# One level's mask and the norm's weights moved from VectorE to ScalarE, the last chunk cut, and a new written order

## The chip, the core and the metric

The kernel runs on one core of a Trainium2 chip. The core has a matmul engine (TensorE, PE in the profile, with its weight loads as PEld), three engines that work on elements (VectorE is DVE, ScalarE is ACT, GpSimd is POOL), and queues that start DMA transfers (most on SyncE, SP; some on POOL). Each engine works through its own list of instructions in order, and they wait for one another by semaphores. The metric is the device time of one execution in microseconds (us); a kernel's time is the median of its runs.

## What is computed

Two parts, one feeding the other. The first is a linear recurrence over 768 positions for 4 x 8 independent heads of width 40. The second is a feed-forward block over the 3072 rows that result:

```python
for t in range(S):
    y[:, :, t] = np.einsum('bhd,bhde->bhe', rt, state)
    Sa = np.einsum('bhde,bhe->bhd', state, at)
    state_decay = state * wt[:, :, None, :] - np.einsum('bhd,bhe->bhde', Sa, bt)
    state = state_decay + np.einsum('bhd,bhe->bhde', vt, kt)
...
rms = np.sqrt(np.mean(x * x, axis=-1, keepdims=True) + 1e-06)
xn = x / rms * rms_g
g = xn @ w_gate
silu = g * (1.0 / (1.0 + np.exp(-g)))
val = xn @ w_val
return silu * val @ w_out
```

The output `y` at position t reads the state before position t is added, so the state after the last position is never read. The rows of x are 320 wide (8 heads of 40), the hidden width is 1536. All data is fp32 on the chip; the weights arrive as 64-bit floats and are converted there.

## The kernel before

**Chunks.** The 768 positions are cut into 24 chunks of 32 (`C`, `NCH`). All 32 heads are worked on together: partitions hold heads and positions, the free dimension holds 16 groups (`NI`) of them. For each chunk c there are three stages.

- `front(c)` (line 676) loads w, a, k, b and v of the chunk, transposes them on PE, and builds for levels of 1, 2, 4, 8 and 16 positions (`LEVELS`) the decayed keys `K`, the decayed factors `Ab` and the products between positions, which masked copies put into `LT`. At the end (lines 775 to 777) it transposes `K` once more, 8 transposes, and ACT copies the result into `KN[32]`, the keys for the update of the state. It also sends `LT` to DRAM and back in another layout, as `M`.
- `inverse(c)` (line 780) solves the triangular system of the chunk on DVE, in 31 pairs of small instructions on `tmp` and `Yi` (62 on DVE for each chunk), and returns the result to `LT` by two DMA steps through `sY`.
- `main(c)` (line 800) uses the state `ST` and the chunk's `LT`: it forms `X`, then the solved values `U`, which go into `VU`; `Sdec` (line 813, 128x640 on DVE) is the decayed state, the 32 products called "update" (line 823) are the new contribution to it, and their sum is the next `ST`. Then come the scores `sc` (32 products, in PSUM), which are masked for each level into `As` (lines 853 to 862), multiplied with the keys of that level (`level`), and combined on DVE from the largest level down into `y` (`down`). Then `y` is transposed, normed (a Square with a sum, a power on POOL, a scaling on ACT), transposed again in three pieces, and written to `xg` with the norm's weights `gcol` (line 920).

The mask `msi` of a level says for each of two halves i of the partitions which positions count. For the largest level (G == 1) and the smallest (l == 1) one DVE instruction on 128x512 elements does both halves, for the three levels between two instructions of 128x256. At the largest level the mask of a half has the same value at all 16 positions.

**Groups.** Two chunks make a group of 64 positions in 4 batches, 256 rows (`CG`, `GT`). `feed(g)` (line 922) is the feed-forward block on a group: 12 slices of 128 hidden columns are loaded (`wf`, by SP), and for each slice PE makes gate and value products into `ps` (of the 320 rows of weights the last 64 by "h64", which needs the third piece of `xg`, the first 256 by "h"), ACT applies Silu (`sg`), DVE multiplies (`hT`), and PE multiplies with the output weights into `po`.

**Weights.** `narrow(f, h)` (line 956) converts the 64-bit weights in 24 half slices at the start, on DVE and ACT, and stores them in DRAM (`sW`), from where every `feed` loads them.

**Order.** What each engine does is not left to a scheduler. All stages only record pieces (a PE piece is a set of products, on other engines a piece is one instruction) in a `Plan`. `Plan.issue` (line 347) then walks through `ORDER`, a text of 6407 words: a number is the place of the next piece among those not yet issued, and "-" stands for one filler, a 128x128 product of the identity into an unused part of `po` (line 1000), which keeps PE's clock up in the first part of the program. `PAIRS` says for each PSUM result which of three buffers `ps` it uses. Each engine's list is its pieces in this order, so the text decides what waits behind what on each engine and on the SP and POOL queues. The two texts were found by a search outside the program; `PRODUCTS`, `LOADS` and the durations in `dve`, `scalar` and so on (in us) are what it planned with.

In the profile nearly all instructions carry the line of a helper: L475 is any DVE instruction, L498 a Silu or other function on ACT, L502 a copy on ACT, L505 a scaling on ACT, L508 the power on POOL, L518 a DMA, L521 a product, L524 a transpose, L1000 a filler.

Of the kernel before, what the change touches and what calls it, by code (L numbers as in the profile page):

```python
# [7 lines left out]
FP32 = mybir.dt.float32  # L8
# [8 lines left out]
P = 128  # L17
C = 32
LEVELS = (1, 2, 4, 8, 16)
CG = 2  # L20
WB = 5
S0, S1 = 15.0, 2.0
LEAD = 2
WARM = 230.0
# [21 lines left out]
36 33 2 26 42 1 31 0 25 343 37 29 107 38 24 36 26 34 262 2 13 1 35 40 0 190 24 339 13 14 - - - 40 17 44 15 41 43 55  # L46
42 8 60 47 175 72 48 45 84 185 59 68 186 585 54 58 - - - - - 49 93 586 53 179 69 71 599 81 176 57 597 50 67 178 609
70 188 80 622 51 92 16 623 65 610 52 56 177 633 64 66 - - - - - - - - - - - - 61 189 9 598 77 79 187 78 587 620 62 0
587 81 - - - - 72 75 179 82 62 90 595 384 194 588 87 11 633 89 589 74 395 620 197 590 380 88 73 195 391 - - - - 101
196 209 390 610 84 102 214 381 201 611 202 5 212 86 213 383 591 85 0 222 92 591 611 17 95 221 224 223 384 94 234 225  # L50
- - 197 233 237 93 391 245 246 592 328 393 198 598 645 612 0 641 598 15 612 592 - 338 205 206 380 642 599 209 0 207
612 200 0 337 612 186 598 6 326 613 2 599 641 34 176 200 216 217 23 600 389 215 33 201 355 95 202 177 96 214 - - - -
211 187 339 93 0 577 0 561 578 297 579 171 192 53 187 191 - - - 182 188 200 623 172 185 625 186 580 562 581 612 355
582 199 1065 197 583 611 183 198 624 184 0 152 1005 850 298 0 298 0 837 295 0 0 0 83 130 298 148 0 298 83 0 507 307
833 0 303 555 0 840 307 0 290 0 67 125 316 314 0 132 125 67 0 0 131 314 0 286 325 0 130 0 298 130 0 291 292 - - - -
- 287 0 293 0 304 0 316 305 301 0 0 283 0 296 0 311 0 322 281 0 286 0 295 280 0 292 - - - - - - - - - - - - - - - -
- 288 0 0 0 0 301 0 285 62 301 116 305 0 283 250 116 0 - - - - - - - - 293 0 258 112 296 0 110 300 256 0 308 307 245
293 292 0 0 304 0 288 0 301 - - - - - - 298 306 0 0 313 0 297 0 0 0 293 310 494 301 0 494 0 302 0 0 299 492 0 0 296
0 246 0 791 0 0 0 787 0 0 93 468 2 796 94 469 0 94 462 794 0 467 93 94 290 461 95 462 96 468 511 97 469 291 98 470
481 289 99 292 471 0 99 100 101 471 102 472 103 481 511 104 482 105 488 106 489 107 483 2 490 108 109 0 293 109 490  # L60
0 108 0 0 379 0 379 387 0 387 369 0 405 378 387 406 0 - - - - - - - - - - - - - - - - - - - - - - - - - - - - - - -
- - - - - - - - - - - - - - - - - - - - - - - - - - - - - - - - - - - - - - - - 44 0 367 377 0 415 0 42 0 414 383 43
412 0 383 410 0 383 40 373 0 0 0 0 0 0 36 0 377 - - - - - - - - - - - - - - - - - 44 0 377 35 44 0 414 0 0 82 0 32 -
43 0 373 0 90 0 229 407 38 88 0 40 78 226 42 38 41 47 48 0 43 226 42 50 45 48 396 0 50 396 43 0 396 0 0 379 395 380
0 395 380 0 401 0 394 0 378 242 400 44 0 400 47 0 145 45 377 242 0 145 391 377 0 216 1 145 391 42 635 398 429 626
146 0 397 39 145 426 634 398 146 147 631 43 623 44 621 45 632 46 148 47 622 - - - - 639 375 376 149 48 416 239 641
830 150 399 377 640 840 0 150 641 653 48 838 151 658 152 645 828 - - - - - - 642 153 670 154 646 155 682 49 656 50
156 669 657 51 157 666 158 667 52 159 643 668 - - - - - - - 53 389 160 161 678 162 1 651 652 - 647 2 702 655 3 654 0
594 610 611 609 625 595 636 109 608 110 596 373 - - - - - - - - - - - 605 590 374 111 345 783 607 626 782 383 112
627 620 622 385 793 113 623 606 375 382 114 792 621 - - - - - - - 617 384 115 376 346 116 377 619 117 635 634 118  # L70
618 378 119 - - - - - 160 633 120 379 121 163 380 161 122 381 123 162 124 164 386 - - - - - - - - - 629 125 387 126
127 128 388 129 630 130 640 631 389 638 131 390 - - - - - 167 641 132 391 133 639 134 392 168 135 393 - - - - - 165
136 394 137 138 430 139 166 571 431 581 643 140 - - - 171 721 644 580 141 642 142 570 143 174 645 144 173 145 178 -
- - 182 175 146 177 147 172 150 149 179 - - - 180 148 637 176 185 732 432 186 433 0 1065 584 283 - 39 1064 36 582 38
284 638 37 40 635 583 0 17 635 480 625 567 497 40 18 624 498 41 284 568 626 42 285 499 627 43 570 286 642 636 44 500
2 706 287 45 643 897 0 493 500 501 643 287 897 656 644 648 2 45 597 907 502 649 494 0 457 860 458 0 613 0 457 611
552 0 - 596 457 621 598 0 622 0 456 595 610 853 457 622 458 634 854 0 505 - - - 500 360 765 521 361 449 531 519 764
504 532 543 362 508 363 0 500 517 543 501 4 515 363 502 364 506 419 514 365 5 366 516 367 0 367 419 368 421 369 370
420 422 44 0 370 - 430 371 44 0 3 40 0 367 426 368 369 370 504 371 37 372 373 374 375 429 376 526 525 521 377 505
522 0 338 466 390 339 397 377 9 340 391 341 392 342 430 393 398 343 480 440 400 378 439 395 387 429 396 394 403 408  # L80
388 0 403 0 342 474 700 403 578 0 700 403 342 709 490 343 0 474 7 696 405 343 709 475 403 344 0 487 706 472 0 485
695 10 343 704 404 0 404 0 4 404 37 405 0 401 31 337 481 402 45 0 474 3 337 338 41 339 402 0 42 3 0 398 705 399 471
50 335 400 898 336 703 470 401 337 37 907 338 339 402 27 480 699 908 704 340 403 341 897 479 486 701 889 343 700 584
478 890 713 714 481 899 702 719 28 706 559 900 342 712 29 560 731 30 0 531 9 0 9 683 684 17 10 0 10 454 0 450 552 10
451 0 10 672 0 672 - - - - - - - - - - - - - - - - 662 25 0 27 670 26 0 682 680 24 695 539 677 676 678 704 661 37 -
- - - 3 36 675 662 296 4 681 434 691 663 679 692 703 672 5 0 0 428 1 680 683 42 682 666 43 687 681 667 20 40 686 21
677 695 2 22 292 0 675 705 287 0 675 287 688 0 671 0 669 665 269 7 17 410 8 682 29 411 412 30 667 413 414 0 8 665 0
675 8 681 672 9 674 0 9 672 - - - - - - - - - - 481 0 9 37 483 411 0 471 0 25 5 401 6 402 403 404 471 7 39 405 473 -
- - - - - - - - - - - 16 0 0 28 8 27 397 0 397 28 0 397 0 654 462 0 5 396 36 8 397 398 37 399 14 47 462 15 0 457 10
723 44 3 11 43 458 583 644 21 12 646 582 4 13 645 461 0 571 21 13 572 458 393 22 14 394 15 466 0 391 455 19 0 372 0  # L90
16 436 0 694 28 5 27 442 6 695 371 439 7 0 696 0 451 370 435 6 760 0 745 0 428 0 741 362 425 0 751 433 362 741 0 748
362 0 425 423 358 733 0 358 0 744 358 432 359 360 0 427 428 0 7 359 0 359 15 0 359 360 6 0 425 0 428 442 359 360 361
362 363 364 0 360 361 742 362 0 362 363 364 419 365 742 366 367 2 368 423 751 369 370 371 372 373 424 675 374 7 0
424 2 0 1154 672 0 1154 421 422 732 432 738 0 669 730 1002 732 670 420 995 731 439 742 685 985 421 0 993 421 687 735
422 686 743 4 1002 423 748 736 991 424 746 983 366 757 367 759 368 425 992 369 744 0 369 746 371 757 755 370 759 768
425 767 736 582 0 582 3 583 584 0 584 751 0 582 746 774 0 731 0 431 737 731 747 421 745 0 731 364 580 0 580 739 581
582 439 583 584 2 424 585 740 757 0 759 740 753 754 760 585 755 586 750 366 587 424 588 365 589 425 364 590 419 591
363 752 592 593 0 347 174 346 175 331 176 342 177 0 177 178 0 178 7 179 342 180 181 359 182 8 183 184 185 186 187
188 189 12 341 190 352 191 192 349 193 194 350 224 195 196 351 0 222 9 224 5 0 4 217 7 0 214 328 335 218 16 332 226
219 343 344 0 417 223 267 338 182 224 266 183 13 184 276 185 0 183 222 184 274 185 186 223 187 330 188 20 189 338 0  # L100
229 223 0 223 188 189 190 191 226 194 227 192 3 225 229 193 224 239 4 0 231 4 0 228 7 233 193 234 238 235 338 339
236 340 532 341 239 12 530 240 194 241 533 195 242 541 197 243 0 538 240 9 608 10 241 536 338 4 13 339 527 242 340
192 539 243 341 342 343 244 0 339 340 240 341 342 0 538 342 240 343 0 16 343 324 344 539 737 345 346 538 727 540 552
# [290 lines left out]
def kernel(  # L394
# [41 lines left out]
    N = 8  # L436
# [116 lines left out]
    for j, l in enumerate(LEVELS):  # L553
        nc.vector.tensor_scalar(iw[:, 2], iw[:, 0], j, None, ALU.logical_shift_right)
        nc.vector.tensor_scalar(msk[:, j], iw[:, 2], 1.0, None, ALU.is_equal)
# [477 lines left out]
```

## Time and profile before

| | |
|---|---|
| median of 5 runs | 1110.35 us (1106.63 to 1112.51) |
| the profiled execution: its time | 1110.35 us |
| its span, from first to last instruction | 1108.5 us |
| granted PE clock, mean over the span | 0.978 |
| products of the first group end, of the last group begin | 265 us, 1062 us |

| row of the profile | count | mean |
|---|---|---|
| DVE As<-ps,msi 128x512 (two levels) | 48 | 683 ns |
| DVE xg<-ps,gcol 128x384 | 24 | 562 ns |
| DVE Sdec<-ST,T 128x640 | 23 | 821 ns |
| PE ps<-ident,K 128x128, all / busy | 192 | 26.4 us |
| PE ps<-VU,KN 64x40, all / busy | 1536 | 20.5 us |
| ACT KN<-ps 128x640 | 96 | 692 ns |
| ACT sg<-ps 128x256 | 144 | 383 ns |
| ACT x<-ps,ss 128x320 (scaled by a column) | 24 | 530 ns |
| ACT Xs<-ps 128x320 (scaled by a number) | 24 | 436 ns |
| PE po<-ident 128x128 (fillers) | 560 | 73.5 us busy |

Each fp32 product is two passes on PE, so a set of 32 products shows as 64, and 280 fillers as 560. A row's busy time is the time in which at least one of its instructions ran; the mean is that of one instruction from start to end, and neighbours overlap. The profile's "idle before" of an engine says how long it stood before such an instruction and which instruction released it. The granted clock is what the throttle allowed PE: 1.00 is full speed, 0.50 half.

### The profile page before, as it was taken

What the parts mean: (1) busy time and instruction counts of PE and PEld (TensorE: products, weight loads), DVE (VectorE), ACT (ScalarE), POOL (GpSimd) and SP (SyncE); (2) the same over time, 40 slices, a digit from 0 to 9 for tenths busy, and PEclk for the clock granted to TensorE, in tenths of its full rate; (3) what the DMA queues carried; (4) which work ended last, traced back from release to release, by engine and by line L of the source; (5) the groups of instructions that cost most, each with busy time, mean ns of one, the idle gap of its engine ahead of it and who ended that gap; (6) DMA issues with size and microseconds to landing.
All of it is one profiled execution on the core that took longest, in us unless ns stands there. A gap on an engine that the chain in (4) does not pass through costs nothing.

```text
span 1108.5 us, 53122 instructions
## 1 busy us (share of the span) xinstructions
PE 1044.8 (94%) x23152; PEld 863.6 (78%) x23152; DVE 906.8 (82%) x3065; ACT 454.5 (41%) x989; POOL 303.2 (27%) x534
## 2 busy tenths in 40 slices
PE   5798889989999999999999999999999999999998
PEld 5697777877878877877777887877878788888876
DVE  5999999899798889789799689989878889798421
ACT  4645554644235235335335335335325335332211
POOL 7520344022223412413422422422304312200000
PEclk9798999989999999999999999999979999999999
DMA  7635554775545636546535545535536535434242
GB/s 158 151 75 155 132 118 123 197 225 142 156 118 128 154 102 145 130 119 153 126 96 142 146 110 150 140 95 153 119 108 149 126 108 151 108 107 130 80 141 79
DMA packets 171177, 145.43 MB, mean 131 GB/s; under 512 B 123712, under 2 KB 142080, under 8 KB 170944
## 3 DMA queue, kind: packets, MB, share of 16 engines
q1 hardware_dynamic: 152576, 119.06, 39.2%
q0 software_dynamic: 16192, 22.64, 10.0%
q8 instruction: 182, 2.98, 1.2%
q10 hardware_dynamic: 2176, 0.33, 0.2%
q14 instruction: 51, 0.42, 0.1%
HBM read 125.83 MB, written 16.12 MB: 128 GB/s over the span
## 4 chain that ended last, share of the span: by engine, by line
PE 64%; DVE 23%; ACT 4%; DMA 3%; issue 3%; POOL 1%; SPq 1%; DVEq 0%; ACTq 0%; POOLq 0%
PE ps L521 43%; PE po L521 11%; PE ps L524 9%; DVE LT L475 3%; DVE tmp L475 3%; DVE Yi L475 3%; DVE K L475 2%; DVE As L475 2%; DVE ex L475 1%; DMA sY<-Yi 1%; DVE wf L475 1%; DVE y L475 1%; ACT K L502 1%; DVE r L475 1%; DVE Ab L475 1%
## 5 line engine op out<-in xcount | busy, mean ns | idle before, releaser
L521 PE MATMUL ps<-xg,wf 128*128 128x256 f32 (+1 forms) x1728 | 357.7, 395 | 2.6 <-DVE xg L475 1.6
L521 PEld LDWEIGHTS ps<-xg,wf 128*128 128x128 f32 (+1 forms) x1728 | 263.2, 190 | 58.1 <-issue 15.2
L521 PE MATMUL po<-wf,hT 128*128 128x320 f32 x576 | 178.6, 444 | 2.9 <-DVE hT L475 1.8
L475 DVE TENSOR_TENSOR tmp<-Yi,M 128x60 f32<-128x60 f32 (+24 forms) x744 | 156.4, 210 | 19.4 <-DMA M<-sB 3.1
L475 DVE TENSOR_TENSOR Yi<-Yi,tmp 128x60 f32<-128x60 f32 (+24 forms) x744 | 155.7, 209 | 15.9
L498 ACT ACTIVATE sg<-ps 128x256 f32<-128x256 f32 x144 | 53.7, 383 | 239.9 <-PE ps L521 222.4
L518 POOL DMA_DIRECT2D VU<-in_v_dram x92 | 53.4, 587 | 354.9 <-PE ps L524 208.2
L521 PEld LDWEIGHTS po<-wf,hT 128*128 128x128 f32 x576 | 102.2, 190 | 39.0 <-issue 3.4
L475 DVE TENSOR_TENSOR hT<-ps,sg 128x256 f32<-128x256 f32 x144 | 59.4, 420 | 54.9 <-ACT sg L498 53.5
L475 DVE TENSOR_TENSOR K<-K,T 128x512 f32<-128x512 f32 (+1 forms) x192 | 93.4, 495 | 10.5 <-PE ps L521 3.8
L521 PEld LDWEIGHTS ps<-Ab,K 40*64 40x64 f32 x4608 | 78.4, 140 | 29.0 <-issue 9.1
L521 PE MATMUL ps<-Ab,K 40*64 40x56 f32 x4608 | 88.3, 226 | 9.4 <-DVE LT L475 2.7
L502 ACT COPY K<-K 128x256 f32<-128x256 f32 (+1 forms) x168 | 71.3, 443 | 61.2 <-PE ps L521 39.6
L475 DVE TENSOR_TENSOR As<-ps,msi 128x256 f32<-128x256 f32 (+1 forms) x192 | 83.3, 482 | 13.0 <-PE ps L521 12.8
L502 ACT COPY KN<-ps 128x640 f32<-128x640 f32 x96 | 66.4, 692 | 55.1 <-PE ps L524 21.6
L521 PEld LDWEIGHTS ps<-As,KN 128*40 128x40 f32 x3072 | 67.1, 125 | 17.4 <-issue 9.4
L521 PE MATMUL ps<-As,KN 128*40 128x32 f32 x3072 | 74.2, 206 | 5.1 <-issue 2.2
L1000 PE MATMUL po<-ident 128*128 128x128 f32 x560 | 73.5, 285 | 5.3 <-ACT po L544 5.3
L518 POOL DMA_DIRECT2D kbn<-in_b_dram x92 | 53.8, 587 | 83.6 <-PE ps L521 73.0
L518 POOL DMA_DIRECT2D wn<-in_w_dram x92 | 51.8, 568 | 85.7 <-DVE tmp L475 32.5
L518 POOL DMA_DIRECT2D kbn<-in_k_dram x92 | 53.4, 584 | 74.3 <-PE ps L521 73.6
L1000 PEld LDWEIGHTS po<-ident 128*128 128x128 f32 x560 | 68.1, 198 | 6.7 <-POOL wan L514 5.2
(124 smaller groups left out, 1549.8 us busy)
## 6 DMA issues: line engine op xcount, KB each, us to landing
wf<-sW SPq DMA_DIRECT2D x144, 480.0 KB, 4.0
M<-sB SPq DMA_DIRECT2D x96, 128.0 KB, 3.8
rn<-in_r_dram SPq DMA_DIRECT2D x24, 160.0 KB, 4.3
sW<-ex SPq DMA_DIRECT2D x16, 240.0 KB, 3.3
out_dram<-o SPq DMA_DIRECT2D x48, 80.0 KB, 3.4
kbn<-in_b_dram POOLq DMA_DIRECT2D x92, 40.0 KB, 3.6
wan<-in_w_dram POOLq DMA_DIRECT2D x46, 80.0 KB, 3.1
wan<-in_a_dram POOLq DMA_DIRECT2D x46, 80.0 KB, 3.3
```

Of the source, the lines that this page charges most:

```text
L475: plan.add("DVE", time + more + each * size(o), 0.087, lambda at: fn(at(o), *m(at)), [o], aps(*args))
L498: scalar(o, [a], lambda at: nc.scalar.activation(at(o), at(a), f, **kw), aps(acc), 0.1 if f in (AF.Square, AF.Relu) else 0.0)
L502: scalar(o, [a], lambda at: nc.scalar.copy(at(o), at(a)), extra=more)
L518: plan.add(by, 0.6 if by == "POOL" else 0.45, 0.0, lambda at: queue.dma_start(out=o, in_=i), [o], [i], load=LOADS[load], since=since)
L521: return o, lhsT, rhs, lambda at: nc.tensor.matmul(at(o), lhsT, rhs, start=start, stop=stop, skip_group_check=True), 4
L524: return o, i, ident, lambda at: nc.tensor.transpose(at(o), i, ident), 2
L1000: plan.warm = lambda: nc.tensor.matmul(po_[:, 0, DM:DM + P], ident, ident, start=False, stop=False, skip_group_check=True)
```

## The change

The masks of the largest level are made by two ACT scalings, one for each half, with one mask value per partition as the factor, in place of one DVE product. The norm's weights are applied by three ACT scalings (one for each piece of 128 columns) in place of one DVE product. In the last chunk, whose new state nobody reads, the 8 transposes and the copy for `KN[32]`, `Sdec` and the 32 update products are no longer recorded. `ORDER` has 6472 words in place of 6407, among them 277 fillers in place of 280, and nearly every line of it is another; `PAIRS` is new too.

There is also a second way of solving the chunk's system in two blocks of 16, used for chunks below `BLOCKS`; `BLOCKS` is 0, so nothing of it is recorded but the constant `lower` (one DVE instruction on 128x1 at the start), and it is cut from the diff here.

```diff
+BLOCKS = 0
...
 ORDER = """
-36 33 2 26 42 1 31 0 25 343 37 29 107 38 24 36 26 34 262 2 13 1 35 40 0 190 24 339 13 14 - - - 40 17 44 15 41 43 55
...
 PAIRS = """
...
@@ front
-        z["KN"][32] = KN_[32].next()
-        copy(z["KN"][32].rearrange("p (n o e) -> p n o e", n=N, o=2),
-             turned(K.rearrange("p (n i) x s -> p n (i x s)", i=2)).rearrange("p n (o e) -> p n o e", o=2)[:, :, :, 0:D])
+        if c + 1 < NCH:
+            z["KN"][32] = KN_[32].next()
+            copy(z["KN"][32].rearrange("p (n o e) -> p n o e", n=N, o=2),
+                 turned(K.rearrange("p (n i) x s -> p n (i x s)", i=2)).rearrange("p n (o e) -> p n o e", o=2)[:, :, :, 0:D])
...
@@ main
-        if c > 0:
+        if 0 < c < NCH - 1:
             tt(Sdec, ST.rearrange("p n i d -> p (n i) d")[:, :, 0:D], z["T"][32].to_broadcast((P, NI, D)), MUL)
...
-        up = plan.room()
-        pe("update", [mm(up[part(o), i, col(slot(n))], kn(z, 32, i, n, o), VU[half(i), n, o, 0:D]) for n, i, o in each])
+        if c + 1 < NCH:
+            up = plan.room()
+            pe("update", [mm(up[part(o), i, col(slot(n))], kn(z, 32, i, n, o), VU[half(i), n, o, 0:D]) for n, i, o in each])
...
-            if G == 1 or l == 1:
-                tt(As[:, j], sc.rearrange("p o n t -> p (o n) t")[:, :, None, 1 if l == 1 else 16:C:2 if l == 1 else 1].to_broadcast((P, NI, 2, 16)),
+            if G == 1:
+                for i in range(2):
+                    scale(As[:, j, :, i], sc.rearrange("p o n t -> p (o n) t")[:, :, 16:C], msi[:, j, i, 0:1])
+            elif l == 1:
+                tt(As[:, j], sc.rearrange("p o n t -> p (o n) t")[:, :, None, 1:C:2].to_broadcast((P, NI, 2, 16)),
                    msi[:, j:j + 1].to_broadcast((P, NI, 2, 16)), MUL)
...
-        tt(xg[c // CG][:, :, c % CG * P:(c % CG + 1) * P], ps, gcol[:, :, None].to_broadcast((P, KT, P)), MUL)
+        for kt in range(KT):
+            scale(xg[c // CG][:, kt, c % CG * P:(c % CG + 1) * P], ps[:, kt], gcol[:, kt:kt + 1])
```

## The prediction

> **What bounds the kernel now.** I read the page's shares first, then the chain that ended last, then the engines in three stretches, then what PE and DVE wait for, and last the one place where PE's clock falls in mid-run.
>
> ```profile
> PE 1044.8 (94%) x23152; PEld 863.6 (78%) x23152; DVE 906.8 (82%) x3065; ACT 454.5 (41%) x989; POOL 303.2 (27%) x534
> PE 64%; DVE 23%; ACT 4%; DMA 3%; issue 3%; POOL 1%; SPq 1%; DVEq 0%; ACTq 0%; POOLq 0%
> ```
>
> PE is busy 94% of the span and carries 64% of the chain, DVE 23%. Those are averages over stretches with different limits, so the span is cut where the first group's products end (265) and where the last group's begin (1062):
>
> ```profile
> 0.00:265.00 265.00, 224.44 (x4868) 196.41 (x4868) 235.43 (x761) 137.78 (x272) 94.28 (x178) 0.94 0.57 149
> 265.00:1062.00 797.00, 779.10 (x18093) 636.24 (x18092) 666.01 (x2293) 311.42 (x705) 208.91 (x356) 0.99 0.49 127
> 1062.00:1108.50 46.50, 41.28 (x192) 30.99 (x192) 5.33 (x13) 5.31 (x14) 0.00 (x0) 0.99 0.36 111
> ```
>
> The columns after the length are PE, PEld, DVE, ACT and POOL busy, then granted clock. In the first stretch PE's 224 contain the 73.5 us of fillers (the row of L1000), and DVE with 235 of 265 is the full engine. In the second PE idles 797 - 779.1 = 17.9 us; DVE has 84%, ACT 39%. In the third PE is alone.
>
> ```profile
> PE ps L521 <- issue: 4.7, 10, 0.9
> PE ps L521 <- DVE LT L475: 2.2, 3, 1.4
> PE ps L524 <- DVE tmp L475: 1.1, 2, 0.6
> PE ps L521 <- DVE xg L475: 1.0, 1, 1.0
> PE ps L521 <- ACT KN L502: 0.9, 2, 0.5
> ```
>
> These are PE's longest waits between 265 and 1062 (total, times, longest). All the rows that name DVE sum to 6.3 us, those that name ACT to 3.8. No single wait is worth much.
>
> ```profile
> 809.82 2.24 DVE L475 COPY_PREDICATED LT<-near,ps 128x384 f32<-128x384 uint32 x3
> ...
> 812.11 1.16 PE L521 MATMUL ps<-Ab,K 40*64 40x56 f32 x64 [1.45 <-DVE LT L475]
> ...
> 800.00:820.00 20.00, 17.83 (x420) 14.44 (x420) 17.18 (x60) 6.62 (x15) 1.02 (x2) 0.86 0.32 102
> 820.00:840.00 20.00, 19.91 (x434) 16.16 (x427) 13.35 (x46) 4.93 (x13) 6.46 (x12) 0.80 0.45 103
> ```
>
> PE stands 1.45 us behind three masked copies on DVE, then 0.19 and 0.53 more, and in rows of 2 us the granted clock is 0.58 at 814 to 816 and 0.50 from there to 828: some 13.6 us at half speed, which cost 13.6 x 0.5 = 6.8 us. It is the only such stretch after 265.
>
> **The change part by part.** Counted in the order of both programs: DVE's recorded instructions go from 3043 to 2994 (24 for the mask, 24 for the norm's weights, one Sdec), ACT's from 968 to 1087 (48 + 72, less one KN copy), and on PE one set of 32 update products and one of 8 transposes are gone. No DMA is added or removed. ORDER and PAIRS are replaced whole, so every queue's sequence moves; SP keeps its 712 transfers and POOL its 460. On SP a weight load that waits for a buffer holds back the LT loads behind it: PE waited 1.4 us for LT<-sY before 265 and not at all after, and I add nothing for a new sequence (the same 1.4 each way).
>
> *Work removed from PE.* In the last chunk 8 transposes of K go (row ps<-ident,K: 26.4 us / 192 x 8 = 1.10 us) and 64 passes of ps<-VU,KN (20.5 / 1536 x 64 = 0.85 us). Both stood between 959 and 1040, where PE idles almost nowhere: -1.95 us. It could shrink to 0 only if PE found nothing ready in their place, and group 10's products are.
>
> *DVE relieved.* Per chunk the 128x512 mask (683 ns) and the 128x384 weights (562 ns): 1.245 us. Up to 265 four chunks' shares go, 5.0 us, from the engine that is full there. The ends are -5.0 (all of it on the path) and +0.5: DVE's waits for ACT in this stretch are 15.2 us, 7.4 of them one early wait, and the other 7.8 grow with ACT's added 8.5 us on 137.8 (6%). The chain there runs through DVE, ACT, DMA and issue by turns, and the PE work ahead of the last filler is the same in both orders (110 us by the trace's durations) with 277 fillers in place of 280, which speaks for little; I take half, -2.5.
> From 265 to 1062 twenty chunks' shares and Sdec (0.82) go: 25.7 us, by which DVE's 131 us of idle time grow by a fifth. PE's waits for it (6.3 us) can fall by nothing or by all; I take the same fifth, -1.3.
>
> *ACT loaded.* A scaling by a column costs 530 ns for 320 elements (x<-ps,ss) against 436 by a number (Xs<-ps), so 94 ns more. A half of the mask, 256 elements, is then 383 + 94 = 0.48, and a third of the weights, 128 elements, 0.30 + 0.09 = 0.39 (Ab<-Ab, 296 ns). Neighbours overlap by 0.1 (two K copies of 0.40 take 0.71), so the mask is 0.86 us against DVE's 0.68, and the weights 0.97 against 0.56. Per chunk that is 0.96 + 1.17 = 2.13 us of ACT, 42.6 us on 311 in the middle stretch (14%).
> For the mask the path hardly changes: between the score products and the first level products the new PE order holds at least 1.8 us of other PE work, as the old one did, and a median of 4.7. If that cover were gone it would cost 0.18 a chunk. For the weights the cover is thin. Between a group's last transposes of x and its first product the old order held 0.0 to 5.6 us of PE work, and 0.0 at two groups, where PE waited (xg: 1.6 us in 2 waits, one ahead of the last group). The new order has no group at 0.0, but eight of twelve at 0.8 to 1.2, against a chain of 0.97. The ends are -1.6 (both waits gone, none new) and 8 x 0.4 = 3.2 less 1.6, or +1.6; I take -0.2. PE's other waits for ACT, 3.8 us, grow with its load: 14%, +0.5 (ends 0 and +3.8).
> What is queued behind the new instructions on ACT are the copies of K, KN and Ab and the activations sg; PE waits for KN, hT and K through them. ACT stood idle 61% of the middle stretch, 181 us of it behind PE for sg, which is the cover.
>
> The Trainium skill speaks against this move: "ScalarE: Activation LUTs", section "Rules for kernel authors", gives multiplications to VectorE. The rows agree on each duration (0.97 against 0.56, 0.86 against 0.68). By the rule the change would lose (0.41 + 0.18) x 24 = 14 us if all were on the path; by the load of the two engines it loses none of that.
>
> *The clock.* A new order has new gaps. The half-speed stretch can vanish (-6.8) or be joined by another (+6.8). I take the fifth by which DVE's slack grows, -1.4. The rule in "TensorE: Matmul & The Clock Gate", section "What's actually happening", is that the clock halves after an idle window of about 3.4 us. Here it fell after 2.2 us of idling in pieces, so the row is stricter than the rule. By the rule no order that keeps PE this full would halve it, and the sum would have -6.8 here.
>
> *Sum.* The profiled execution took 1110.35 us, span 1108.5 and 1.85 around it, and it is also the median of the five runs (1106.63 to 1112.51). -1.95 - 2.5 - 1.3 - 0.2 + 0.5 - 1.4 = -6.85, so 1103.5 us.
>
> **The rivals.** *More half-clock stretches (slower).* Place: the middle stretch, wherever the new order leaves PE some 2 us without work. Price: 6.8 for the clock and 2.2 for the gaps, 9.0 each. From 1103.5 + 1.4, one more than before gives 1113.9 and two 1122.9; I write 1118. It decides from the first extra one. For it: a single wait of 1.45 was enough, and every gap is new. Against: DVE, which made that gap, gets lighter.
> *ACT's queue becomes the wait (slower).* The new scalings wait on PE at ACT's head and hold back a copy of 0.40 in each chunk: 24 x 0.40 = 9.7 us against -1.95 and -2.5, so 1115.6. For it: ACT waits for PE longer than for anything else, and it works in order. Against: 61% idle, and at least 1.8 us of cover at the mask.
> *DVE was never the limit (same).* Only PE's removed work comes out: 1110.35 - 1.95 = 1108.4. For it: the middle stretch is PE's, and the fillers are nearly as many. Against: DVE at 89% up to 265, 23% of the chain.
> That the change does less than it says can be left aside: BLOCKS is 0, so the block inverse is not recorded, and the counts above are those of the words.
>
> **How the numbers follow.** Forecast 0.56, more half-clock 0.22, ACT's queue 0.08, DVE no limit 0.14. The predicted time is the forecast's 1103.5. Its own range is 1095 (start 5.0, all DVE waits, half the clock stretch: -1.95 - 5.0 - 6.3 - 3.4 = -16.6, with +1.2 for ACT) to 1109. The range given is 1095 to 1117, which takes in the ACT case and one extra stretch and leaves out two, and about a tenth below. What a measurement can tell from no change is about 0.3%, 3.3 us: faster is below 1107.0, slower above 1113.7. Faster: 0.53 from the forecast, 0.05 from the PE-only case, 0.58. Slower: most of the clock's 0.22 and half of ACT's, 0.26. The rest, 0.16, is same.
>
> **What would show it.** In the new profile: DVE busy near 907 - 30.7 = 876, ACT near 454.5 + 51 - 0.7 = 505, and PE near 1042. Up to the end of the first group's products (265 before) the start should take about 262; if it still takes 265, DVE was no limit there. PE's waits for xg should be small and many, not two large ones, and now name ACT. The granted clock between 265 and 1062 should dip once or not at all. What would make this wrong: a second or third dip there, PE idle in the middle stretch above 20 us, or waits of PE for ACT of 10 us and more.

## The result and the profile after

The changed kernel took 1112.99 us (median of 53 runs, 1103.83 to 1119.16), the kernel before on the same chips 1109.27 us (95 runs): a ratio of 1.0032, 95% interval 1.0021 to 1.0043. It is 3.7 us slower, where 6.85 us less had been forecast. The profiled execution of the changed kernel took 1110.23 us (span 1108.1, mean granted clock 0.983), 2.8 us under its own median: over its 54 recorded executions 0.01 of mean clock goes with 6.5 us (7.5 us for the kernel before), and at a clock of 0.98 the two stand at 1113.2 and 1109.7 us. The two profiled executions took the same time, so the traces show what is different inside, not the 3.7 us.

The page of the changed kernel: engine shares, the DMA queue of kind "instruction" (packets, MB, share), and the chain's shares by engine:

```profile
PE 1041.3 (94%) x23074; PEld 858.7 (77%) x23074; DVE 887.5 (80%) x3017; ACT 487.4 (44%) x1108; POOL 302.7 (27%) x534
...
q8 instruction: 181, 2.97, 1.1%
...
PE 65%; DVE 20%; issue 5%; ACT 4%; DMA 3%; POOL 2%; SPq 1%; DVEq 0%; POOLq 0%; ACTq 0%
```

DVE lost 19.3 us of busy time (the instructions that went had 30.7 us of durations, all durations together fell by 28.4; overlaps make the rest), PE 3.5. On the chain DVE gave up 3 points, and "issue" took 2 of them. The three stretches of the changed kernel, columns as before:

```profile
0.00:265.00 265.00, 221.21 (x4856) 193.54 (x4857) 232.79 (x749) 141.78 (x292) 93.92 (x178) 0.95 0.58 149
265.00:1062.00 797.00, 778.85 (x18032) 634.38 (x18031) 649.80 (x2257) 339.85 (x803) 208.75 (x356) 0.99 0.50 127
1062.00:1108.10 46.10, 41.25 (x188) 30.82 (x188) 4.91 (x12) 5.77 (x14) 0.00 (x0) 0.97 0.37 110
```

PE's busy time in the middle is what it was (778.85 against 779.1), though the last chunk's work is gone from it. PE's longest waits there, changed kernel:

```profile
PE ps L524 <- issue: 8.1, 11, 1.9
PE ps L524 <- DVE Yi L478: 1.5, 3, 0.7
PE po L524 <- issue: 1.3, 1, 1.3
PE ps L524 <- DVE hT L478: 0.8, 2, 0.6
PE ps L524 <- DVE tmp L478: 0.7, 2, 0.5
```

The rows that name DVE now sum to 4.6 us (6.3 in the prediction's count), those that name ACT to 3.0; the rows with no releaser, "issue", grew from 6.0 to 9.4. The clock dips after 265 are three short ones (10.2 us at half speed in all, near 774, 785 and 819) in place of one of 13.7. The first two follow at once on waits of PE with no releaser (1.94 us before 774.1, 1.11 before 784.1). The first group's products end at 266.8 (265.2 before).

The largest new hole lies in the start. The stretch around 200 in the kernel before, then in the changed kernel (us, then PE, PEld, DVE, ACT, POOL busy, granted clock, DMA share, GB/s):

```profile
197.00:200.00 3.00, 3.00 (x29) 3.00 (x28) 2.50 (x6) 2.75 (x6) 0.00 (x0) 1.00 0.60 178
200.00:203.00 3.00, 2.89 (x78) 2.62 (x76) 2.97 (x9) 1.38 (x5) 0.00 (x0) 1.00 0.69 210
203.00:206.00 3.00, 3.00 (x18) 2.13 (x16) 2.90 (x9) 0.12 (x1) 0.00 (x0) 1.00 0.35 90
```

```profile
197.00:200.00 3.00, 0.04 (x2) 0.00 (x0) 2.68 (x7) 2.19 (x4) 0.00 (x0) 1.00 0.90 275
200.00:203.00 3.00, 2.28 (x78) 2.10 (x78) 2.56 (x8) 0.89 (x2) 0.00 (x0) 0.66 0.61 183
203.00:206.00 3.00, 3.00 (x14) 2.00 (x12) 2.97 (x9) 1.41 (x5) 0.00 (x0) 0.50 0.58 168
```

PE stands for 3 us, and then its clock is halved for 7 us. What it waits for is the subject of the last experiments.

### The profile page after: what moved, and what is told of

It reads as the page before. It is cut to its first block, busy times and chain, and to the rows that moved or that the text cites. A ratio compares the mean times of both kernels' runs of the same rounds, so it can differ in the third digit from the quotient of the medians.

```text
span 1108.1 us, 53038 instructions
## 1 busy us (share of the span) xinstructions
PE 1041.3 (94%) x23074; PEld 858.7 (77%) x23074; DVE 887.5 (80%) x3017; ACT 487.4 (44%) x1108; POOL 302.7 (27%) x534
## 3 DMA queue, kind: packets, MB, share of 16 engines
q8 instruction: 181, 2.97, 1.1%
## 4 chain that ended last, share of the span: by engine, by line
PE 65%; DVE 20%; issue 5%; ACT 4%; DMA 3%; POOL 2%; SPq 1%; DVEq 0%; POOLq 0%; ACTq 0%
PE ps L524 44%; PE po L524 12%; PE ps L527 8%; DVE tmp L478 3%; DVE LT L478 3%; DVE Yi L478 3%; DVE ex L478 2%; DVE y L478 2%; DVE K L478 2%; DVE As L478 1%; DVE wf L478 1%; SPq L521 1%; DVE Ab L478 1%; POOL kbn L521 1%; DMA wf<-in_moe_w_out_dram 1%
## 5 line engine op out<-in xcount | busy, mean ns | idle before, releaser
L521 POOL DMA_DIRECT2D VU<-in_v_dram x92 | 53.3, 586 | 363.9 <-PE ps L527 229.3
L505 ACT COPY KN<-ps 128x640 f32<-128x640 f32 x95 | 65.6, 692 | 55.5 <-PE ps L527 21.4
L521 POOL DMA_DIRECT2D kbn<-in_b_dram x92 | 53.6, 586 | 99.6 <-PE ps L524 99.6
L524 PEld LDWEIGHTS ps<-As,KN 128*40 128x40 f32 x3072 | 64.8, 123 | 18.1 <-issue 13.9
L478 DVE TENSOR_TENSOR As<-ps,msi 128x256 f32<-128x256 f32 (+1 forms) x168 | 68.5, 455 | 11.0 <-PE ps L524 8.9
L524 PE MATMUL ps<-As,KN 128*40 128x32 f32 x3072 | 71.5, 204 | 4.1 <-issue 3.0
L521 POOL DMA_DIRECT2D wn<-in_w_dram x92 | 51.6, 566 | 86.6 <-DVE KN L478 39.1
L521 POOL DMA_DIRECT2D kbn<-in_k_dram x92 | 53.7, 587 | 51.1 <-PE ps L524 43.6
```

Source lines behind the costliest of these rows:

```text
L478: plan.add("DVE", time + more + each * size(o), 0.087, lambda at: fn(at(o), *m(at)), [o], aps(*args))
L505: scalar(o, [a], lambda at: nc.scalar.copy(at(o), at(a)), extra=more)
L521: plan.add(by, 0.6 if by == "POOL" else 0.45, 0.0, lambda at: queue.dma_start(out=o, in_=i), [o], [i], load=LOADS[load], since=since)
L524: return o, lhsT, rhs, lambda at: nc.tensor.matmul(at(o), lhsT, rhs, start=start, stop=stop, skip_group_check=True), 4
```

## The experiments

Names: b_ kernels are the kernel before with an edit, n_ kernels the changed kernel with one. A part that is added or undone is put into the written order at the place of the instruction that it replaces; all else keeps its place. Ratios are against the kernel before on the same chip, with 95% intervals.

**Each part undone in the new order.**

```diff
 n_maskdve: the changed kernel, the mask of the largest level on DVE
-for i in range(2): scale(As[:, j, :, i], ...sc[16:C], msi[:, j, i, 0:1])
+tt(As[:, j], ...sc[16:C].to_broadcast(...), msi[:, j:j + 1].to_broadcast(...), MUL)
 n_xgdve: the norm's weights on DVE
-for kt in range(KT): scale(xg[...kt...], ps[:, kt], gcol[:, kt:kt + 1])
+tt(xg[...], ps, gcol[:, :, None].to_broadcast((P, KT, P)), MUL)
 n_order: both
```

> The changed kernel with its new order, but the largest level's mask is again one DVE product (at the place of the first of its two ACT scalings). Theory M (the mask's scalings on ACT lose: ACT and DVE read the same PSUM buffer one at a time, in the changed trace ACT stands 28.8 us behind DVE's masks): the loss of 3.7 us goes, about 1107 us, ratio 0.997 to 1.000 to the kernel before. Theory O (the new order itself loses): stays near 1113, ratio 1.002 to 1.004. Theory X (the norm's weights on ACT lose): stays near 1113. ACT's waits for DVE's As fall to 0 in any case.

> The changed kernel with its new order, but the norm's weights are again one DVE product (at the place of the first of the three ACT scalings). Theory X: back to 1109 or below. Theories M and O: stays near 1113, ratio 1.002 to 1.004.

> The changed kernel's order and shortened last chunk, with both the mask and the norm's weights back on DVE. Theories M and X: 1106 to 1109, that is the kernel before less the 1.95 us of PE work. Theory O: 1112 or more. If DVE's relief was worth something in this order, this is slower than the one with only the mask put back.

Measured: n_maskdve 1.0092 [1.0063, 1.0121], n_xgdve 1.0076 [1.0051, 1.0101], n_order 1.0147 [1.0118, 1.0176]. In the new order each part on ACT is worth having: 0.6% for the mask, 0.44% for the weights, 1.15% for both. None of the theories had expected n_maskdve and n_xgdve above 1113 us. So the loss against the kernel before is not in the two moves as such; the order, with the work where it was, is 1.5% worse. That is a price for work which this order was not made for; the same work in both orders is compared further down.

**Each part alone in the old order.** The same edits on the kernel before, forwards; b_cut is only the shortened last chunk, b_all all three.

> The kernel before with its own order and only the last chunk shortened (8 transposes, a KN copy, Sdec and 32 update products left out; their words taken out of the order). All theories: PE loses 1.95 us of work, so 1107 us, ratio 0.998. If it stays at 1109 the removed work was filled by idling.

> The kernel before with its own order and only the largest level's mask as two ACT scalings (at the place of the DVE product). In the new order this mask on ACT is worth 6.7 us (0.32% against 0.92%). Theory O (the parts gain, the new order loses): 1102 to 1107, ratio below 0.998. Rival F (an order fits the engines it was found for, any single move loses in it): ratio above 1.002, since ACT's queue has no room made for it.

> The kernel before with its own order and only the norm's weights as three ACT scalings (at the place of the DVE product). Theory O: below 0.998. Rival F: above 1.002; two groups have no PE work between the last transposes and the first product, so PE's waits for xg grow by 0.4 us at each.

> The kernel before with its own order and all three parts: mask and weights on ACT, last chunk shortened. This is the change without the new order. Theory O: 1098 to 1104, ratio 0.990 to 0.995. Rival F: 1112 or more. DVE busy near 887, ACT near 487 as in the changed kernel.

Measured: b_cut 0.9991 [0.9969, 1.0014], b_mask 1.0033 [1.0012, 1.0053], b_xg 1.0040 [1.0015, 1.0064], b_all 1.0088 [1.0065, 1.0111]. The cut gives about 1 us or nothing. In an order that was not made for them, both moves lose, as rival F had it. For the weights PE's waits show it; the longest between 265 and 1062 in b_xg:

```profile
PE ps L519 <- ACT xg L503: 4.8, 10, 1.1
PE ps L519 <- DVE LT L473: 2.2, 3, 1.4
```

All of PE's waits for ACT after 265 grew from 3.8 to 10.2 us. For the mask it is ACT and DVE that wait for one another. In b_mask, among DVE's and ACT's own waits:

```profile
DVE As L473 <- ACT As L503: 22.1, 21, 4.0
ACT As L503 <- DVE As L473: 15.0, 12, 2.0
```

and in the changed kernel, where ACT's turn comes after DVE's:

```profile
ACT As L508 <- DVE As L478: 28.8, 19, 4.6
```

DVE was to save 16 us by the mask; in b_mask it stands 22 us for ACT (its waits for PE at the masks fall from 12.8 to 7.3). In none of the 24 chunks of the changed kernel do the two engines' masks overlap, though they work on different levels; in 21 chunks one engine begins 0.03 to 0.10 us after the other's end.

**Why the two take turns.** Both read the scores in PSUM and write parts of one tile `As`. n_sep writes the largest level into a tile of its own.

```diff
-As_ = Turns(1, [P, len(LEVELS), NI, 2, 16], "As")
+As_ = Turns(1, [P, len(LEVELS) - 1, NI, 2, 16], "As")
+As16_ = Turns(1, [P, NI, 2, 16], "Ah")
...
-scale(As[:, j, :, i], ...)
+scale(Ah[:, :, i], ...)
```

> The changed kernel with the largest level's mask written to a tile of its own, the others to theirs. If ACT waits for DVE's masks because they write one tile, the 28.8 us of waiting vanish; if because both read one PSUM buffer, they stay and so does the time, near 1113 (ratio 1.003).

> The changed kernel unaltered, beside the kernel before on one chip. The variant with a tile of its own for the largest mask has the same instructions and waits as this and measured 0.9998. If the kernel's loss holds on any chip: ratio 1.002 to 1.004. If chips differ: 0.998 to 1.001.

Measured: n_sep 0.9998 [0.9973, 1.0023], the changed kernel unaltered once more (after_again) 1.0023 [1.0005, 1.0042]. ACT's waits in n_sep:

```profile
ACT Ah L508 <- DVE As L478: 28.7, 19, 4.6
```

The wait is the same, so it is not the written tile. What the two engines still share is the PSUM buffer `sc` and the table of masks `msi`; no run separates these. n_sep has the changed kernel's instructions and nearly its waits, so it is a second sample of it, and the gap between its ratio and the 1.0032 says what twelve runs can tell. The Trainium skill has a rule that points to `sc`: "PSUM — Partial Sum Buffer", section "PSUM bank collisions raise a hardware error", says that two engines may not be on the same bank and quadrant at once, two reads included, and that the compiler keeps them apart by a dependency. The waits here agree with it.

**The mask left out.** After the first chunk the largest level is not masked anew: b_nomask in the old order, n_nomask in the new one.

```diff
 b_nomask
-tt(As[:, j], ...sc[16:C].to_broadcast(...), msi[:, j:j + 1].to_broadcast(...), MUL)
+if c == 0: tt(As[:, j], ...sc[16:C].to_broadcast(...), msi[:, j:j + 1].to_broadcast(...), MUL)
 n_nomask
-for i in range(2): scale(As[:, j, :, i], ...)
+for i in range(2 if c == 0 else 0): scale(As[:, j, :, i], ...)
```

> The kernel before in its own order, the largest level's mask left out from the second chunk on (23 DVE products of 0.683 us gone, nothing put on ACT; that level's product then reads the first chunk's masked scores). What freeing DVE of the mask is worth at most. If DVE limits: 16 us less DVE work gives 1100 to 1106. If PE limits and DVE's relief is worth nothing: 1108 to 1110, ratio 0.998 to 1.001.

> The changed kernel in its order, with the largest level's mask left out from the second chunk on (46 ACT scalings gone; that level's product reads the first chunk's). What the two scalings and ACT's 29 us of waiting behind DVE's masks cost in the changed kernel. If they are its loss: 1108 to 1109 or less, ratio below 1.000. If they are hidden: as the changed kernel beside it, within 1 us.

Measured: b_nomask 0.9973 [0.9952, 0.9994], n_nomask 1.0031 [1.0016, 1.0047]. With 16 us less on DVE the old order gains 3.0 us. In the new one, leaving out ACT's scalings and their 28.8 us of waiting gains nothing against after_again: there they are covered, as the prediction had it.

**The same work in two orders.** b_neither and n_neither have the cut, no mask of the largest level after the first chunk and no weights after the second group: every engine has the same work but for 3 of 280 fillers (0.8 us). nb_start has n_neither's order up to the end of the first group's products and b_neither's after it, nb_half up to the fifth group. b_tail is b_cut with the new order from the middle of group 9 on.

```diff
 b_neither, n_neither: beside the mask as in b_nomask
-tt(xg[...], ps, gcol[...], MUL)
+if c < 2 * CG: tt(xg[...], ps, gcol[...], MUL)
 nb_start, nb_half
+order of n_neither: pieces 0 to the end of the first group's products (nb_start), or through the fifth group (nb_half)
+order of b_neither: all pieces not yet issued, as they stand there
```

> All work on the engines of the kernel before, last chunk shortened, its own order up to the middle of group 9's products and the new order for what is left after that. In the traces the stretch after group 10's last product is 44.9 us in the new order and 47.0 in the old. So 1.95 and 2.1 us less: 1105 us, ratio 0.996. If the shorter end is paid for before it: 0.998 to 1.000, as with the last chunk shortened alone.

> Old order, with both moved pieces of work left out of the kernel before: the largest level's mask from the second chunk on, the norm's weights from the third group on (the later groups' products read old rows), and the last chunk shortened. What is left on every engine is the same as in the next run. With the mask left out the old order measured 0.9973; less the cut's 0.1% and less the waits for the weights: 1103 to 1106, ratio 0.993 to 0.996.

> The new order, with the same work left out (largest mask from the second chunk on, norm's weights from the third group on, last chunk shortened). Same instructions on every engine as the run beside it, only the order differs. Theory R (the order of all the rest is worse, 6 us, by what it was bent to make room on ACT or by chance): 5 us or more above the run beside it, ratio 0.999 to 1.003. Theory W (the weights on ACT cost what is left, the rest of the order is as good): within 2 us of the run beside it.

> The same work left out; the new order up to about the end of the first group's products, the old order from there. Under R: if the new order's start loses, 1 to 3 us above the old order's run; if the loss is in the steady part, level with it.

> The same work left out; the new order up to the end of the fifth group's products, the old order from there. Under R with a loss spread over the groups: about half way between the old and the new order's runs. If one end holds it: level with one of them.

Measured: b_neither 0.9960 [0.9936, 0.9984], n_neither 1.0065 [1.0038, 1.0091], nb_start 1.0056 [1.0029, 1.0083], nb_half 1.0064 [1.0034, 1.0094], b_tail 0.9982 [0.9956, 1.0007]. The same work costs 1116.0 us in the new order and 1105.1 in the old, 10.9 us more, and a kernel that takes only its start from the new order is as slow. Neither expectation for nb_start (1 to 3 us, or level) holds. Yet most of its loss does not fall in the start. In the profiled executions the groups' products end at (us):

| group | 1 | 5 | 6 | 7 | 8 | 11 | 12 |
|---|---|---|---|---|---|---|---|
| b_neither | 267.3 | 589.0 | 669.3 | 754.0 | 832.4 | 1057.0 | 1099.0 |
| nb_start | 270.0 | 591.2 | 679.1 | 763.7 | 846.9 | 1072.1 | 1113.7 |
| n_neither | 268.9 | 588.1 | 671.9 | 752.0 | 837.7 | 1071.5 | 1111.6 |

nb_start is 2.7 us behind after the first group, 2.2 after the fifth, and 9.8 after the sixth, though from 278 us on its PE list is that of b_neither. In the sixth group it stands where b_neither runs through (first two lines nb_start, third b_neither):

```profile
614.11 0.38 PE L515 MATMUL ps<-VU,KN 64*40 64x40 f32 x18 [1.27 <-issue]
623.85 1.49 PE L515 MATMUL ps<-rE,vut 40*64 40x32 f32 x43 [3.86 <-issue]
615.82 1.09 PE L516 MATMUL ps<-rE,vut 40*64 40x32 f32 x64
```

After the second wait the clock is halved for 7 us. Another 4.8 us come in the eighth group, with 13 us at half clock that b_neither does not have (the kernel before, b_mask, b_xg, b_all and b_tail have it there too).

With both parts gone from DVE (and not put on ACT) the old order gains 4.4 us: DVE's relief is worth something. b_tail is the fastest kernel here that does the whole work, but its interval holds 1.

**What the new start waits for.** In every kernel with the new start, and in none with the old, PE stands 2.5 to 5.1 us near 200. In the changed kernel the 128x128 product on DVE that finishes `A`, which PE needs next, stands behind seven weight conversions. n_early1 moves this one instruction ahead of them; n_early3 also moves the last additions of `y` near 112 and one `hT` near 251, where PE waited 3.8 and 2.2 us.

```diff
 DVE near 196 in the changed kernel, and in n_early1
-K K K o wf ex T wf o ex T wf A
+K K K A o wf ex T wf o ex T wf
```

> The changed kernel with one instruction moved in its order, nothing else: the DVE product of 128x128 that finishes A of chunk 5 is issued ahead of the seven weight conversions and two T products that stand before it on DVE. In the changed kernel PE waits 3.7 us for it near 200 and the granted clock is then half for some 7 us. If the new order loses by what DVE's list puts ahead of PE's operands at the start, the wait near 200 falls from 3.1-3.7 to under 1 us, the clock holds there, the first group's products end 3 to 6 us earlier (261 to 264 in place of 266.8), and the ratio falls from 1.002-1.003 to 0.997-1.000. If DVE's total load sets the end of the start, the conversions that were pushed back make PE wait elsewhere, the first group still ends at 266 to 268 and the ratio stays at 1.002-1.003.

> As n_early1, and two more places of the changed kernel's start: near 112 the five DVE additions and products that finish y of chunk 0 are issued ahead of the weight conversions before them (with one conversion on ACT put behind two copies), where PE waits 2.7-3.8 us for y, and near 251 one hT product is issued some 8 DVE instructions earlier, where PE waits 2.2 us for it. PE, SP and POOL keep their order. If waits behind DVE's list are the loss, each removed wait comes out in part, the first group's products end at 257 to 262 and the ratio is 0.991 to 0.997, below the kernel before; if the load of DVE sets the end, it ends at 265 to 268 and the ratio stays within 1.000 to 1.004.

Measured: n_early1 1.0025 [0.9993, 1.0056], n_early3 1.0003 [0.9978, 1.0029]; the first group's products end at 269.0 and 267.6. Both miss what the theory of DVE's list expected. n_early3 comes out as its rival had it, that DVE's load sets the end of the start; but in b_nomask DVE has 2 us less to do by then and the first group still ends at 265.0. In n_early3 the wait for `y` is gone, but PE waits in its place between 109 and 122 for

```profile
PE ps L520 <- ACT K L501: 2.4, 1, 2.4
PE ps L523 <- ACT Ab L501: 2.1, 1, 2.1
```

and in place of 2.2 us for `hT` near 251 it waits 4.0 us for `hT` near 245: there a wait that is taken away comes back elsewhere. And the wait near 200 did not move at all. It was not for `A`. PE in the changed kernel, then in n_early1 (start, us, what, idle before and its releaser):

```profile
194.75 0.79 PE L524 MATMUL ps<-ST,aP 40*32 40x40 f32 x64
195.47 0.91 PE L524 MATMUL ps<-VU,LT 32*32 32x40 f32 x64
...
200.11 0.22 PE L524 MATMUL ps<-r,Sd 40*40 40x32 f32 x1 [3.08 <-issue]
...
201.06 1.97 PE L524 MATMUL ps<-A,K 40*64 40x56 f32 x64 [0.61 <-DVE A L478]
```

```profile
201.81 0.27 PE L520 MATMUL ps<-r,Sd 40*40 40x32 f32 x1 [2.62 <-issue]
```

Of the 3.7 us only 0.61 were for `A`, and those went. The other 3.08 stand in the midst of a set of products that had been running since 196.3, and the profile names no releaser.

**What "issue" is.** The trace gives it away by counting. Seven of the longer waits of this kind in the changed kernel stand before products 3775, 4539, 6951, 10130, 16484, 16739 and 19153 of PE's list; the steps are 764, 2412, 3179, 6354, 255 and 2414, which are 6, 19, 25, 50, 2 and 19 times 127.1. The queue of kind "instruction" shown above moved 2.97 MB in 181 packets, 16.4 KB each, and 23074 products over 181 packets are 127.5 a packet. Counted together with the weight loads, which PE's list holds as well, it is sharper: all 15 such waits of the kernel before, and 17 of the 19 of the changed one, stand at the same place in steps of 256 (193 or 194 after a multiple of it), and 16384 bytes are 256 times 64. So PE's program arrives in packets of some 127 products, and these are the places where one packet ends. The trace's packet times around 200 (us):

```
               packet starts  landed   its first product   PE idle before it
before             196.80     197.84        200.98               none
changed            197.26     198.76        200.11               3.08
n_early1           199.45     200.59        201.81               2.62
```

Taken over all packets, one starts 1.0 us (median) after PE has entered the packet before it, lands 1.0 us later, and at these 17 stalls of the changed kernel PE went on 1.2 to 1.5 us after the landing. A packet is thus as a rule fetched one ahead, and these three times make some 3.3 us. That is no sharp limit, because one packet in twenty starts about 3 us or more after PE has entered the one before it: of the packets that the changed kernel used up in under 3.3 us, 8 of 14 were followed by a stall (3 of 11 in the kernel before); of those that lasted 3.3 to 4 us, 3 of 20 (5 of 25); of the longer ones, 5 of 145 (7 of 143). In the old order the packet before the one at 200 took PE 6.3 us: a set of 64, four large products, 32 passes of fillers. In the new order three sets of 64 small products follow one another from 194.75 on, and 1.8 us were enough to use the packet up.

PE's waits with no releaser over the whole span, kernel before and changed kernel:

```profile
PE ps L521 <- issue: 7.7, 13, 1.4
PE po L521 <- issue: 1.0, 1, 1.0
PE ps L524 <- issue: 0.3, 1, 0.3
```

```profile
PE ps L524 <- issue: 15.7, 17, 3.1
PE po L524 <- issue: 1.3, 1, 1.3
PE ps L527 <- issue: 0.4, 1, 0.4
```

9.0 and 17.4 us, of which 9.0 and 16.8 lie at ends of packets. Over the 20 kernels of this study (one profiled execution each):

| | kernels | PE's "issue" waits, whole span | up to 269 us |
|---|---|---|---|
| start of the old order | 8 | 5.0 to 11.7 us | 2.5 to 5.8 us |
| start of the new order | 12 | 14.5 to 21.2 us | 5.5 to 10.4 us |

The two groups do not overlap in the whole span. nb_start shows how a start can do this to what follows: its list from 278 us on is the old one, but with another number of products and waits ahead of it the packets end at other products, and after 269 us it has 10.0 us of such waits against 6.5 in b_neither. The Trainium skill, "Runtime: NRT & Kernel Launch", section "Instruction fetch mechanics", has the program fetched in 16 KiB blocks of 256 instructions, the next one while the current one runs, and calls the cost of crossing a block mostly hidden. Size, number and manner agree with the packets; "mostly hidden" does not hold here: PE stands 9.0 us at their ends in the kernel before, 16.8 in the changed one.

No kernel was run in which only these waits were taken away (with small and large products mixed again in the new start, for example), and the profiles do not show that they are the whole loss. From the kernel before to the changed one they grow by 8.4 us, but PE's other waits shrink by 5.3, so that its idle time goes from 63.7 to 66.8 us. In n_neither against b_neither they grow by 8.8 us, and PE's idle time even falls, from 66.7 to 65.6 us; that profiled pair is 12.6 us apart because PE's clock is lower (0.972 against 0.985), more than the means of all their runs are (0.9796 against 0.9823). What is shown is that the new order costs PE these waits, and that halved clock follows the longest of them. That they are most of the loss is likely, not shown.

## Why the prediction was wrong, step by step

**The step that failed** is the treatment of the new order outside the places it was asked about. For the queue the prediction says "I add nothing for a new sequence"; for PE it priced the cover at the mask and the weights and the gaps that halve the clock, and took all else as equal. The sum has no term for what the order itself costs. With the same work on every engine the new order takes 10.9 us longer (n_neither against b_neither), which is more than all that was to be gained. The row that would have asked the question was shown: "PE ps L521 <- issue: 4.7, 10, 0.9" stands at the head of PE's waits; the prediction summed the rows that name DVE and ACT and passed over this one, the largest. These waits, PE's waiting for its program, grow by 7.8 us (9.0 to 16.8 at ends of packets), 4.2 to 4.6 of them in the start in three samples. Put into the prediction's sum without its clock term, -5.45, they make +2.3; the mean clock of the runs (0.9806 against 0.9811) adds 0.4; measured are +3.7. That comes near, but it counts the waits in full, while in the profiles PE's other waits shrink beside them. So the order is shown to be the loss; how much of it is the waiting for the program stays open.

**PE's removed work, -1.95:** b_cut measured -1.0 us [-3.4, +1.6]; consistent, not resolved.

**DVE relieved, -2.5 and -1.3:** the instructions that went had the 30.7 us forecast; busy time came to 887.5 in place of 876. What that is worth in the old order: b_neither gains 4.4 us [1.8, 7.1], less 1.0 for the cut 3.4, against 3.8. The size agrees, but not the place where it should show. The prediction said that DVE was no limit up to there if the first group still ended at 265 in place of 262; it ended at 266.8, 265.8 and 268.9 in three samples of the changed kernel, and with the mask gone from the old order at 265.0 (b_nomask). The half of 5.0 us that was taken for the start is not seen; the old order's own samples of that start spread from 265.2 to 267.1. n_early3 hints why the start gives little: a wait that goes comes back elsewhere.

**ACT, +0.3 in all:** durations were right (a third of the weights 368 ns against 0.39, half a mask 472 against 0.48), busy time came to 487 in place of 505 because neighbours overlapped more. In the new order the cover for the mask held (n_nomask gains nothing). PE's waits for ACT in the middle, 3.0 us, did not grow, and none of them is for `xg`. But the cover was read as a matter of time alone: that ACT and DVE take turns at the scores was missed. In the new order that cost nothing; in the old order the mask on ACT cost 0.33%, and the weights 0.40%.

**The clock, -1.4:** three short dips came in place of one, and "a second or third dip there" was the prediction's own first sign of being wrong. Two of them follow waits for the program. They are shorter, and in the mean of many runs the clock is nearly the same, so 0.4 us the other way.

**The rivals.** Slower it was, but by none of the three. More half-clock stretches: their place was to be the middle, and there they shrank; the new one at 200 is in the start and follows a wait for the program. ACT's queue as the limit: PE's waits for it are in b_xg, not in the changed kernel. DVE never the limit: b_nomask, n_maskdve and n_order speak against it.

## What to carry to other kernels

When a written order is replaced, every row of PE's waits counts, also the one with no releaser: see whether these waits stand at equal steps in the engine's list, and compare the queue of kind "instruction". Sets of many small products side by side can use up the program faster than it arrives (here 127 of them in 1.8 us); large products or fillers between them gave the next packet time, 6.3 us at the same place in the old order. A part moved to another engine is to be tried without its order redone and with it: here each move lost 0.3 to 0.4% in the old order and gained 0.4 to 0.6% in one made for it, which says that neither engine loads nor durations alone price such a move. And an edit early in the list shifts the ends of all later packets, so two kernels that differ only in their start can differ anywhere.

## What was not expected of the hardware

PE's program is fetched while it runs, in packets of 16.4 KB, as a rule one ahead. PE often stalls when it has used up a packet of 127 products in less than some 3.3 us (8 of 14 times in the changed kernel), in one kernel for up to 21.2 us in all and 5.1 at once, and the clock was halved after waits of 1.1 to 5.1 us of this kind. Two engines that read one PSUM buffer did not overlap in any chunk (28.8 us of waits on ACT). Executions of one kernel spread by about 3 us (standard deviation), and about half of that variance goes with the mean granted clock, some 7 us for 0.01.
